# Moving the memory products of a gated attention kernel to the ends of its projection tiles, and making one of them from float32r halves

## The chip, the cores and the metric

The kernel runs on one core of one Trainium2 chip. A core has five engines that each work through a queue of their own in order: TensorE (PE, with its weight loads shown apart as PEld), VectorE (DVE), ScalarE (ACT), GpSimd (POOL) and SyncE (SP), which here only issues DMAs. Work on different engines is ordered by semaphores. The metric is the device time of one execution in microseconds.

## The reference: what is computed

For an input x of 2048 rows and 512 columns the reference computes two attentions with 32 heads of size 16 each, and mixes their outputs with a sigmoid gate per row.

```python
g = _sigmoid((x * gate_w).sum(-1, keepdims=True))
a = _A_ref(x, A_wqkv, A_wo)                 # full softmax attention over all 2048 rows
b = _B_ref(x, B_wq, B_wk, B_wv, B_wo, B_beta)
return g * a + (1 - g) * b
```

Side B works in four segments of 512 rows. Within a segment it is causal-block softmax attention; beside that each head keeps a memory M (16 x 16) and z (16) over the earlier segments:

```python
pq = phi(qs)                                 # phi(t) = t + 1 where t > 0, else exp(t)
num = jnp.einsum("bhld,bhde->bhle", pq, M)
den = jnp.einsum("bhld,bhd->bhl", pq, z)[..., None] + 1e-6
o = g * (num / den) + (1.0 - g) * a_dot      # this g is sigmoid(beta), per head
pk = phi(ks)
M = M + jnp.einsum("bhld,bhle->bhde", pk, vs)
z = z + jnp.einsum("bhld->bhd", pk)
```

The change concerns these memory products and two small loads: the gate's weights (`gw`) and `beta`.

## The kernel before

The program has two parts. The first projects x to queries, keys and values of side A, then of side B, and keeps the memory. The second, from line 700 on, makes scores, exponentials, values and the output, and runs for most of the time.

The first part is laid out by hand in *slots*. A call of `slot` (L304) issues the 12 matmuls of one projected tile of 128 rows by 512: four depth steps with three products each, because every operand is split into a high and a low float32r half (float32r is float32 rounded so that TensorE multiplies it in one pass; the low half holds the rest). After every three matmuls comes a *place*, 0 to 3, where other work is issued that was posted for this slot and this place with `post(slots, place, f)` (that many slots from now) or `post_at`. Work of one place is issued in the order in which it was posted. Since every engine's queue is in order, a place fixes where an instruction stands in the queue of its engine.

Side B takes twelve slots for each chunk c of 512 rows: q tiles in slots 12c to 12c+3, v tiles in 12c+4 to 12c+7, k tiles in 12c+8 to 12c+11. The texts below count these slots from the first one of side B. `qk_tile` (L362) posts three steps for the slot after a tile's matmuls: `e0` at place 0 (ScalarE copies the bank to `full` and casts it to the half `q1`, GpSimd makes `mn`, the minimum with 0), `e1` at place 1 (VectorE makes the low half `q2`, ScalarE `ex` = exp(mn)), `e2` at place 2 (VectorE makes `ph`, that is phi). Then, for a tile o of four:

- `mem_q` (L508), two slots after the q tile at place 1, multiplies phi(q) with the block-diagonal memory `mbd`, a float32 product `num` on TensorE; ScalarE copies it to `am`, and SyncE sends it away. After the fourth tile `mem_den` (L518) makes `den` a slot later at place 1.
- `mem_k` (L530), two slots after the k tile at place 1, transposes phi(k) on TensorE (`tps`), ScalarE copies that to `pt`; `mem_k2` (L538) at place 3 of the same slot makes the product `mps` with the values; `mem_k3` (L546) at place 0 of the next slot adds it on VectorE to the running `mrun` and makes `mbd` and `zbd`.

The banks of `num`, `den`, `tps` and `mps` come from one pool of two PSUM banks, `me_ps`, handed out in turn. `pt` and `am` share one buffer.

The second part needs the row maxima of the scores. The first 96 parts of them are made early, in the first part: `some_max` (L556) stands at place 3 of slots 14 to 19, 24 to 31 and 36 to 45, ahead of what is posted there later, and issues four maxima products `sm` on TensorE, which use half of its rows each, into four banks, with a reduction each on VectorE (L226). When the 64 maxima of the first side A unit are done, `finish_max` (L179) turns them with `nm` on VectorE and two `ms` operations on GpSimd. `gate_logit` (L471) is a VectorE product `jk` for the output gate, four for each chunk; its scratch is the buffer of `mn`.

Query tiles of the second part come from the pool `qp` (L94) with six buffers; three units are loaded in the first part. `gw` and `beta8` are loaded by GpSimd's DMA queue at the start (L454, L456).

Of the kernel before, what the change touches and what calls it, by code (L numbers as in the profile page):

```python
# [10 lines left out]
F32 = mybir.dt.float32  # L11
F32R = mybir.dt.float32r
# [7 lines left out]
D = 512  # L20
H = 32
DH = 16
CH = 512
NCH = S // CH
KT = D // 128
NG = 8
NO = 4
# [20 lines left out]
def gated_mix(ctx, tc, x, xT, wqkv, a_wo, b_wq, b_wk, b_wv, b_wo, beta, gate_w, out):  # L48
    nc = tc.nc
# [29 lines left out]
    bmask = const.tile([128, 8, DH], F32, name="bmask")  # L79
# [7 lines left out]
    gh = const.tile([128, NO], F32, name="gh")  # L87
# [189 lines left out]
    with ExitStack() as p0:  # L277
# [23 lines left out]
        def post(slots, place, f):  # L301
            posted.setdefault((now[0] + slots, place), []).append(f)
# [13 lines left out]
        def post_at(n, place, f):  # L316
            posted.setdefault((n, place), []).append(f)
# [133 lines left out]
        wAk = halves(wp, "wk", wqkv[:, D:2 * D], None, 2, [None, pairs[0]])  # L451
        wAv = halves(wp, "wv", wqkv[:, 2 * D:3 * D], 1, 4, [early[1].rearrange("p (k d) -> p k d", k=2), pairs[1]])
        gw = wk1.tile([128, D], F32, tag="gw", name="gw")
        nc.gpsimd.dma_start(gw, gate_w.unsqueeze(0).broadcast_to([128, D]))  # L454
        beta8 = wk1.tile([8, NO], F32, name="beta8")
        nc.gpsimd.dma_start(beta8, beta.rearrange("(o h) -> h o", h=8))  # L456

        def betas():

# [39 lines left out]
            xc = xn  # L499

        mrun = [st.tile([128, 8, 17], F32, name=f"mrun{o}") for o in range(NO)]
        mbd = [st.tile([128, DH, 8], F32, name=f"mbd{o}") for o in range(NO)]
        zbd = st.tile([128, NO, 32], F32, name="zbd")
        nc.gpsimd.memset(zbd, 0.0)

        pqs = []

        def mem_q(o, c, pq):  # L508
            nps = me_ps.tile([128, CH], F32, tag="me", name="num")
            nc.tensor.matmul(nps, mbd[o].rearrange("p e h -> p (e h)"), pq, start=True, stop=True)  # L510
            am = wk.tile([128, CH], F32, tag="am", name="am", bufs=1)
            nc.scalar.copy(am, nps)
            nc.sync.dma_start(numd[c][:, o], am)
            pqs.append(pq)
            if o == NO - 1:
                post(1, 1, lambda: mem_den(c))

        def mem_den(c):  # L518

            dps = me_ps.tile([128, CH], F32, tag="me", name="den")  # L520
            for o in range(NO):
                nc.tensor.matmul(dps[32 * o:32 * o + 32], zbd[:, o], pqs[o], start=True, stop=True,
                                 tile_position=(0, 32 * o))
            pqs.clear()
            dn = wk1.tile([128, CH], F32, tag="dn", name="dn")
            nc.scalar.activation(dn, dps, AF.Identity, bias=eps)
            for o in range(NO):
                nc.sync.dma_start(dend[c][8 * o:8 * o + 8], dn[32 * o:32 * o + 8])

        def mem_k(o, c, pk, vs):  # L530
            tps = me_ps.tile([128, 4, 128], F32, tag="me", name="tps")
            for b in range(4):
                nc.tensor.transpose(tps[:, b], pk[:, b * 128:(b + 1) * 128], identf)
            pt = wk.tile([128, CH], F32, tag="am", name="pt", bufs=1).rearrange("p (b t) -> p b t", t=128)
            nc.scalar.copy(pt, tps)
            post(0, 3, lambda: mem_k2(o, c, pt, vs))

        def mem_k2(o, c, pt, vs):  # L538
            mps = me_ps.tile([128, 8, 17], F32, tag="me", name="mps")
            for b in range(4):  # L540
                nc.tensor.matmul(mps.rearrange("p (g h) e -> p g (h e)", g=2), pt[:, b],
                                 vs[:, 2 * o:2 * o + 2, b].rearrange("p g h e -> p g (h e)"),
                                 start=(b == 0), stop=(b == 3))
            post(1, 0, lambda: mem_k3(o, c, mps))

        def mem_k3(o, c, mps):  # L546
            if c == 0:
                nc.vector.tensor_copy(mrun[o], mps)
            else:
                nc.vector.tensor_add(mrun[o], mps, mrun[o])  # L550
            nc.vector.scalar_tensor_tensor(mbd[o].rearrange("p e h -> p h e"), mrun[o][:, :, 0:16], gh[:, o:o + 1], bmask,
                                           op0=ALU.mult, op1=ALU.mult)
            nc.vector.tensor_scalar_mul(zbd[:, o, 0:8], bmask[:, :, 0], mrun[o][:, 0, 16:17])


# [29 lines left out]
        for c in range(NCH):  # L585
            if c + 1 == NCH:
                load_gate(c)
                post(8, 2, gates)
            for o in range(NO):
                then = (lambda pq, o=o, c=c: post(1, 1, lambda: mem_q(o, c, pq))) if c else None  # L590
                qk_tile("B", wBq, xc, o, qd["B", o, c], then)
            if c + 1 < NCH:
                xn = halves(xp, "x", xchunk(c + 1), now[0], now[0] + 3)
            if c + 1 < NCH:
                post(2, 3, lambda c=c: load_gate(c))
            vs = v_tiles("B", wBv, xc, c)
            for o in range(NO):
                then = (lambda pk, o=o, c=c, vs=vs: post(1, 1, lambda: mem_k(o, c, pk, vs))) if c + 1 < NCH else None
                qk_tile("B", wBk, xc, o, kd["B", o, c], then)
            xc = xn  # L600
        while posted:
# [491 lines left out]
```

## Time and profile before

| what | value |
|---|---|
| median of 3 runs | 1781.45 us (1780.76 to 1781.96) |
| profiled execution | 1781.19 us |
| its span in the trace | 1779.4 us |
| first projection matmul | 6.2 us |
| side B's projections and memory products, with the early maxima | about 117 to 303 us |
| second part | from 303.6 us |
| TensorE busy in the span | 1770.9 us (100%) |
| VectorE / ScalarE / GpSimd busy | 88% / 81% / 36% |

Times of instructions are us from the start of the span. A timeline row gives the start, the duration, the engine, the line, the operation, out<-in and the count; in brackets stands the idle time of the engine before it and what ended that. Matmuls are pipelined, so their durations overlap: what a matmul costs is read from start to start. In the stage views each engine has its busy time and, in parentheses, its instructions.

### The profile page before, as it was taken

What the parts mean: (1) busy time and instruction counts of PE and PEld (TensorE: products, weight loads), DVE (VectorE), ACT (ScalarE), POOL (GpSimd) and SP (SyncE); (2) the same over time, 40 slices, a digit from 0 to 9 for tenths busy, and PEclk for the clock granted to TensorE, in tenths of its full rate; (3) what the DMA queues carried; (4) which work ended last, traced back from release to release, by engine and by line L of the source; (5) the groups of instructions that cost most, each with busy time, mean ns of one, the idle gap of its engine ahead of it and who ended that gap; (6) DMA issues with size and microseconds to landing.
All of it is one profiled execution on the core that took longest, in us unless ns stands there. A gap on an engine that the chain in (4) does not pass through costs nothing.

```text
span 1779.4 us, 40691 instructions
## 1 busy us (share of the span) xinstructions
PE 1770.9 (100%) x14945; PEld 912.0 (51%) x14945; DVE 1573.8 (88%) x3331; ACT 1436.8 (81%) x2752; POOL 641.6 (36%) x748
## 2 busy tenths in 40 slices
PE   9999999999999999999999999999999999999999
PEld 7887776444444444444444444444444444444444
DVE  4235777999999999999999999999999999999931
ACT  5455444888888888888888888888888888888884
POOL 3002222405161416443434343343434253425342
PEclk9999999999999999999999999999999999999999
DMA  7677556444453536554454545454535354534551
GB/s 248 214 231 244 186 196 190 122 110 134 120 160 106 144 112 176 146 141 133 131 139 123 146 128 146 128 146 122 152 105 160 113 140 117 155 110 141 142 163 61
DMA packets 141270, 261.55 MB, mean 147 GB/s; under 512 B 36328, under 2 KB 58888, under 8 KB 140560
## 3 DMA queue, kind: packets, MB, share of 16 engines
q1 hardware_dynamic: 139712, 257.55, 49.9%
q8 instruction: 119, 1.95, 0.5%
q0 software_dynamic: 1216, 1.14, 0.3%
q14 instruction: 79, 0.65, 0.1%
q10 hardware_dynamic: 144, 0.26, 0.1%
HBM read 174.39 MB, written 83.25 MB: 145 GB/s over the span
## 4 chain that ended last, share of the span: by engine, by line
PE 94%; DVE 2%; ACT 1%; DMA 1%; POOL 1%; issue 0%; SPq 0%; POOLq 0%; DVEq 0%
PE ops L797 33%; PE st L740 27%; PE sm L205 14%; PE pr L311 10%; PE ops L909 4%; PE ops L680 2%; PE sm L909 2%; POOL mn L378 1%; PE pr L401 1%; DVE pm L226 1%; PE num L510 0%; DMA qdB<-q 0%; ACT ex L385 0%; DVE q L381 0%; PE mt_ps L196 0%
## 5 line engine op out<-in xcount | busy, mean ns | idle before, releaser
L763 ACT ACTIVATE p<-st 128x512 f32<-128x512 f32 x2261 | 1189.2, 600 | 152.8 <-PE sm L205 105.9
L226 DVE TENSOR_REDUCE pm<-sm 128x1 f32<-128x512 f32 x2048 | 1280.4, 681 | 11.8 <-PE sm L205 11.6
L740 PE MATMUL st<-qA,kA 50*128 50x512 f32 x2014 | 663.3, 432 | 0.0
L205 PE MATMUL sm<-kA,qA 48*128 48x512 f32 x2048 | 659.0, 428 | 0.1
L797 PE MATMUL ops<-p,vA 128*17 128x128 f32 (+3 forms) x6432 | 551.9, 441 | 0.0
L740 PEld LDWEIGHTS st<-qA,kA 50*128 50x128 f32 x2014 | 327.5, 185 | 415.2 <-ACT p L763 371.2
L205 PEld LDWEIGHTS sm<-kA,qA 48*128 48x128 f32 x2048 | 330.5, 185 | 15.3 <-issue 7.1
L859 POOL TENSOR_TENSOR rcp<-rec,minus 128x32 f32<-128x32 f32 x43 | 234.3, 5449 | 75.9 <-DMA rec<-dend 71.3
L238 DVE CUSTOM_DVE_ANT_0 rest<-sm,mask 128x128 f32<-128x128 f32 (+3 forms) x512 | 246.8, 482 | 1.8 <-PE sm L205 0.5
L797 PEld LDWEIGHTS ops<-p,vA 128*17 128x17 f32 x6432 | 130.4, 96 | 215.4 <-issue 190.4
L744 POOL TENSOR_SCALAR_AFFINE_SELECT p<-p 128x512 f32<-128x512 f32 x128 | 79.7, 640 | 330.3 <-ACT p L763 325.9
L205 PE MATMUL sm<-kB,qB 48*128 48x128 f32 (+3 forms) x512 | 166.1, 384 | 0.0
L740 PE MATMUL st<-qB,kB 50*128 50x512 f32 (+1 forms) x495 | 109.2, 329 | 0.3 <-ACT mt L199 0.3
L381 DVE TENSOR_TENSOR q<-full,q 128x512 fp32r<-128x512 f32 x56 | 38.6, 689 | 75.3 <-ACT q L374 68.8
L740 PEld LDWEIGHTS st<-qB,kB 50*128 50x128 f32 x495 | 69.8, 186 | 59.5 <-ACT p L763 48.7
L797 PE MATMUL ops<-p,vB 128*17 128x128 f32 (+3 forms) x1504 | 87.5, 350 | 0.0
L205 PEld LDWEIGHTS sm<-kB,qB 48*128 48x128 f32 x512 | 79.9, 184 | 0.0
L187 POOL CAST ms<-nm 128x16 fp32r<-128x16 f32 x32 | 6.7, 210 | 201.3 <-DVE nm L183 199.4
L378 POOL TENSOR_SCALAR mn<-full 128x512 f32<-128x512 f32 x24 | 35.7, 1489 | 101.3 <-ACT full L373 80.9
L373 ACT COPY full<-pr 128x512 f32<-128x512 f32 x56 | 32.7, 584 | 42.9 <-PE pr L311 39.2
L187 POOL CAST ms<-pm 128x16 fp32r<-128x16 f32 x32 | 6.3, 198 | 128.4 <-DVE pm L238 128.3
L875 POOL TENSOR_TENSOR v<-v,inv 128x512 f32<-128x512 f32 x31 | 39.9, 1289 | 27.2 <-DMA inv<-rdA 23.6
(198 smaller groups left out, 1617.5 us busy)
## 6 DMA issues: line engine op xcount, KB each, us to landing
kA<-kdA SPq DMA_DIRECT2D x256, 128.0 KB
vA<-vdA SPq DMA_DIRECT2D x31, 544.0 KB
kA<-kdA SPq DMA_DIRECT2D x256, 64.0 KB
kdA<-q SPq DMA_DIRECT2D x32, 256.0 KB
qdB<-q SPq DMA_DIRECT2D x32, 256.0 KB
qA<-qdA SPq DMA_DIRECT2D x64, 128.0 KB
kdB<-q SPq DMA_DIRECT2D x32, 256.0 KB
qB<-qdB SPq DMA_DIRECT2D x64, 128.0 KB
```

The source lines that it names most:

```text
L205: nc.tensor.matmul(ps[:, n0:n0 + n], rows(qt[u][:, :, s * 128:(s + 1) * 128], h, 48), rows(k[:, :, k0:k0 + n], h, 48), start=True, stop=True)
L226: nc.vector.tensor_reduce(pm[:, h, s, kc:kc + 1], ps, axis=AX.X, op=ALU.max)
L238: rows_left.append(lambda h=h, s=s, n0=n0, w=w: nc.vector.tensor_tensor_reduce(out=tri["rest"][:, 0:w], in0=ps[:, n0:n0 + w], in1=tri["mas ...
L311: nc.tensor.matmul(ps, l(a, k), r(b, k), start=(n == 0), stop=(n == 11))
L378: nc.gpsimd.tensor_scalar_min(ph["mn"], full, 0.0)
L740: nc.tensor.matmul(ps[:, n0:n0 + CH - q0], rows(k[:, :, b * 128:(b + 1) * 128], h, 50), rows(q[:, :, q0:], h, 50), start=True, stop=True)
L744: nc.gpsimd.affine_select(out=x, in_=x, pattern=[[0, 4], [1, 128]], base=0, channel_multiplier=-1, compare_op=ALU.is_ge, fill=0.0)
L763: nc.scalar.activation(p[:, h], ps, AF.Exp, scale=SCALE)
L797: nc.tensor.matmul(ops[32 * h:32 * h + 17, q0:q0 + 128 * w], v[:, 17 * h:17 * h + 17], p[:, h, c0:c0 + 128 * w], start=(i == 0), stop=done ...
L859: eng.tensor_tensor(r, rec, minus, op=ALU.pow)
L875: eng.tensor_mul(k["v"], k["v"], k["inv"])
L909: yield lambda i=i, x=x, w=w: nc.tensor.matmul(ps, t[:, b, x], halved[side][:, o, w], start=start and i == 0, stop=stop and i == 2)
```

## The change

- `mem_den`, `mem_k` and `mem_k2` move to place 3: `den` from place 1 to place 3 of the slot after the last `num`, `tps` from place 1 to place 3 of its slot, and `mps` to place 3 of the slot after that (so `mem_k3` is a slot later too). Posted during the run of the slots, they stand behind `some_max`, which was posted before; `beside_max` posts `tps` in two steps, so that `mps` of a tile stands ahead of `tps` of the next.
- `num` is made from halves. For every q tile, a new step `halve_q` two slots after it at place 1 lets ScalarE cast phi(q) to a high half and GpSimd subtract that for the low half; `mem_q` follows three slots after the tile at place 2, with three float32r matmuls in place of one float32 product. `mem_k3` splits `mbd` on VectorE: one copy and one subtraction of 128 x 128 more. The halves lie in three buffers of `qp`; `mbd` is one tile for all four o.
- `beta8` is loaded at slot 8 and `gw` at slot 16 of the first part's count (from the first slot of side A).

```diff
--- before.py
+++ after.py
@@ -451,9 +451,9 @@
         wAk = halves(wp, "wk", wqkv[:, D:2 * D], None, 2, [None, pairs[0]])
         wAv = halves(wp, "wv", wqkv[:, 2 * D:3 * D], 1, 4, [early[1].rearrange("p (k d) -> p k d", k=2), pairs[1]])
         gw = wk1.tile([128, D], F32, tag="gw", name="gw")
-        nc.gpsimd.dma_start(gw, gate_w.unsqueeze(0).broadcast_to([128, D]))
         beta8 = wk1.tile([8, NO], F32, name="beta8")
-        nc.gpsimd.dma_start(beta8, beta.rearrange("(o h) -> h o", h=8))
+        post_at(8, 0, lambda: nc.gpsimd.dma_start(beta8, beta.rearrange("(o h) -> h o", h=8)))
+        post_at(16, 0, lambda: nc.gpsimd.dma_start(gw, gate_w.unsqueeze(0).broadcast_to([128, D])))
 
         def betas():
 
@@ -499,21 +499,34 @@
             xc = xn
 
         mrun = [st.tile([128, 8, 17], F32, name=f"mrun{o}") for o in range(NO)]
-        mbd = [st.tile([128, DH, 8], F32, name=f"mbd{o}") for o in range(NO)]
+        mbd = st.tile([128, DH, 8], F32, name="mbd")
+        pqh = [qp.tile([128, 2, CH], F32R, tag="q", name="pqh") for _ in range(2)]
+        mbh = qp.tile([128, 2, CH], F32R, tag="q", name="mbh").rearrange("p a (o m) -> p a o m", o=NO)
         zbd = st.tile([128, NO, 32], F32, name="zbd")
         nc.gpsimd.memset(zbd, 0.0)
 
         pqs = []
 
+        def beside_max(f):
+
+            post(0, 3, lambda: post(1, 3, f))
+
+        def halve_q(o, pq):
+            ph = pqh[o % 2]
+            nc.scalar.copy(ph[:, 0], pq)
+            nc.gpsimd.tensor_sub(ph[:, 1], pq, ph[:, 0].bitcast(F32))
+
         def mem_q(o, c, pq):
             nps = me_ps.tile([128, CH], F32, tag="me", name="num")
-            nc.tensor.matmul(nps, mbd[o].rearrange("p e h -> p (e h)"), pq, start=True, stop=True)
+            ph = pqh[o % 2]
+            for i, (a, b) in enumerate(((0, 0), (1, 0), (0, 1))):
+                nc.tensor.matmul(nps, mbh[:, a, o], ph[:, b], start=i == 0, stop=i == 2)
             am = wk.tile([128, CH], F32, tag="am", name="am", bufs=1)
             nc.scalar.copy(am, nps)
             nc.sync.dma_start(numd[c][:, o], am)
             pqs.append(pq)
             if o == NO - 1:
-                post(1, 1, lambda: mem_den(c))
+                post(1, 3, lambda: mem_den(c))
 
         def mem_den(c):
 
@@ -533,7 +546,7 @@
                 nc.tensor.transpose(tps[:, b], pk[:, b * 128:(b + 1) * 128], identf)
             pt = wk.tile([128, CH], F32, tag="am", name="pt", bufs=1).rearrange("p (b t) -> p b t", t=128)
             nc.scalar.copy(pt, tps)
-            post(0, 3, lambda: mem_k2(o, c, pt, vs))
+            post(1, 3, lambda: mem_k2(o, c, pt, vs))
 
         def mem_k2(o, c, pt, vs):
             mps = me_ps.tile([128, 8, 17], F32, tag="me", name="mps")
@@ -548,8 +561,11 @@
                 nc.vector.tensor_copy(mrun[o], mps)
             else:
                 nc.vector.tensor_add(mrun[o], mps, mrun[o])
-            nc.vector.scalar_tensor_tensor(mbd[o].rearrange("p e h -> p h e"), mrun[o][:, :, 0:16], gh[:, o:o + 1], bmask,
+            nc.vector.scalar_tensor_tensor(mbd.rearrange("p e h -> p h e"), mrun[o][:, :, 0:16], gh[:, o:o + 1], bmask,
                                            op0=ALU.mult, op1=ALU.mult)
+            m = mbd.rearrange("p e h -> p (e h)")
+            nc.vector.tensor_copy(mbh[:, 0, o], m)
+            nc.vector.tensor_sub(mbh[:, 1, o], m, mbh[:, 0, o].bitcast(F32))
             nc.vector.tensor_scalar_mul(zbd[:, o, 0:8], bmask[:, :, 0], mrun[o][:, 0, 16:17])
 
 
@@ -587,7 +603,7 @@
                 load_gate(c)
                 post(8, 2, gates)
             for o in range(NO):
-                then = (lambda pq, o=o, c=c: post(1, 1, lambda: mem_q(o, c, pq))) if c else None
+                then = (lambda pq, o=o, c=c: (post(1, 1, lambda: halve_q(o, pq)), post(2, 2, lambda: mem_q(o, c, pq)))) if c else None
                 qk_tile("B", wBq, xc, o, qd["B", o, c], then)
             if c + 1 < NCH:
                 xn = halves(xp, "x", xchunk(c + 1), now[0], now[0] + 3)
@@ -595,7 +611,7 @@
                 post(2, 3, lambda c=c: load_gate(c))
             vs = v_tiles("B", wBv, xc, c)
             for o in range(NO):
-                then = (lambda pk, o=o, c=c, vs=vs: post(1, 1, lambda: mem_k(o, c, pk, vs))) if c + 1 < NCH else None
+                then = (lambda pk, o=o, c=c, vs=vs: beside_max(lambda: mem_k(o, c, pk, vs))) if c + 1 < NCH else None
                 qk_tile("B", wBk, xc, o, kd["B", o, c], then)
             xc = xn
         while posted:
```

## The prediction

> **What bounds the kernel now.** I read the page's chain first, then the busy times by stage, then the first part's TensorE timeline.
>
> ```profile
> span 1779.4 us, 40691 instructions
> PE 94%; DVE 2%; ACT 1%; DMA 1%; POOL 1%; issue 0%; SPq 0%; POOLq 0%; DVEq 0%
> ```
>
> TensorE carries 94% of the chain. All that is changed stands in the first part, whose three hand-overs (k tiles of a chunk, then q tiles of the next) are these stages:
>
> ```profile
> core 0: us, PE busy (x) PEld busy (x) DVE busy (x) ACT busy (x) POOL busy (x), PEclk, DMA share, GB/s
> 139.20:188.50 49.30, 48.77 (x233) 35.09 (x233) 32.47 (x63) 26.71 (x47) 12.21 (x9) 1.00 0.69 222
> 188.50:239.10 50.60, 50.28 (x242) 35.53 (x240) 38.13 (x73) 23.66 (x42) 12.17 (x9) 1.00 0.54 183
> 239.10:290.60 51.50, 50.99 (x245) 35.68 (x243) 39.53 (x80) 22.35 (x40) 12.96 (x11) 1.00 0.58 187
> ```
>
> TensorE is at the wall in each, but VectorE is at 39.53 of 51.50 us in the last, and its work stands in bunches. The second part starts when the first ends and has nothing changed; whatever is won or lost is won or lost before 304 us.
>
> **What TensorE is spared.** The product `num`, now (start, duration, operation):
>
> ```profile
> 163.56 1.02 PE L510 MATMUL num<-ph,mbd 128*128 128x512 f32 x2
> 164.65 0.40 PE L311 MATMUL pr<-xl,wqh 128*128 128x512 f32 x1
> 164.88 0.39 PE L311 MATMUL pr<-xh,wqh 128*128 128x512 f32 x1
> ```
>
> A projection matmul of 128x512, also float32r, takes 0.23 us from start to start (164.65 to 164.88). From 163.56 to 164.65 are 1.09; less one projection that is 0.86 for `num`. Three float32r matmuls are 3 x 0.23 = 0.69. Twelve times 0.17 is 2.1 us less.
>
> The second term is waiting: `tps` in mid-tile comes before phi(k) is ready.
>
> ```profile
> 154.38 0.40 PE L311 MATMUL pr<-xh,wqh 128*128 128x512 f32 x1
> 155.25 0.63 PE L533 MATMUL tps<-identf,ph 128*128 128x128 f32 x4 [0.47 <-DVE ph L390]
> 155.95 0.39 PE L311 MATMUL pr<-xl,wqh 128*128 128x512 f32 x1
> 159.19 0.39 PE L311 MATMUL pr<-xh,wqh 128*128 128x512 f32 x1
> 160.09 0.39 PE L311 MATMUL pr<-xl,wqh 128*128 128x512 f32 x1
> ...
> PE tps L533 <- DVE ph L390: 1.1, 3, 0.5
> PE num L510 <- DVE ph L390: 0.2, 1, 0.2
> ```
>
> Between the outer projections of the first `tps` lie 1.57 us, of the second, which waits for nothing, 0.90: the wait costs 0.67 where the row says 0.47. The waits' list (us in total, times, longest) has 1.1 for three such, so about 1.6 on the path, one in each hand-over; `num` adds about 0.3 once. Two places and a group of maxima later, phi(k) is long there.
>
> Third, `den` goes behind the maxima:
>
> ```profile
> 281.12 0.39 PE L311 MATMUL pr<-wkh,xh 128*128 128x512 f32 x1
> 282.44 0.39 PE L311 MATMUL pr<-wkl,xh 128*128 128x512 f32 x1
> ...
> 283.37 0.40 PE L311 MATMUL pr<-wkh,xh 128*128 128x512 f32 x1
> 285.03 0.40 PE L311 MATMUL pr<-wkl,xh 128*128 128x512 f32 x1
> ...
> 276.29 0.40 PE L311 MATMUL pr<-wkh,xh 128*128 128x512 f32 x1
> 277.28 0.41 PE L196 MATMUL mt_ps<-identf,ms 128*32 128x128 f32 x2
> 277.95 0.40 PE L311 MATMUL pr<-wkl,xh 128*128 128x512 f32 x1
> ```
>
> Less two projections each (0.46), the maxima alone (281.12 to 282.44) cost 0.86, `den` (283.37 to 285.03) 1.20, and maxima followed by `mt_ps`, tiled in columns as `den` is, 1.20. So a small column-tiled group still pays 0.34 behind the maxima, and `den` there saves some 0.1 at most: 0.3 for three. `tps` and `mps` only change places. Nothing more is saved at the switch.
>
> Fourth, at the start, `gw` (256 KB) leaves the crowd of the first loads:
>
> ```profile
> 0.80 4.71 DMA raw<-wqkv
> 1.95 0.84 POOL L454 DMA_DIRECT2D gw<-gate_w  x1
> ```
>
> TensorE's first projection waits for that load. The issue of `gw` starts 1.15 us behind it, and 0.84 more goes into issuing, so it shares at most 5.51 - 2.79 = 2.7 of the 4.7 us. At an equal share with the four 256 KB loads that SyncE and ScalarE had issued by then, a fifth of that, 0.5, is the upper end; 0 is the lower. I take 0.2, since its data cannot flow at once. `beta`'s few bytes, and both later DMA issues on GpSimd's queue (0.84 us, ahead of nothing timed; used tens of us later), I cost at nothing. In sum, if nothing else binds: 2.1 + 1.6 + 0.3 + 0.3 + 0.2 = 4.5 us.
>
> **What is late next.** Four prices stand against it. The first is a bank. `mps` of a tile takes the bank that `mps` of the tile before leaves, which is free when VectorE has done `mrun`. That now stands a slot later in VectorE's queue, behind the gate's `jk`:
>
> ```profile
> 152.53 0.63 ACT L385 ACTIVATE ex<-mn 128x512 f32<-128x512 f32 x1 [0.84 <-POOL mn L378]
> 153.20 0.69 DVE L473 SCALAR_TENSOR_TENSOR jk<-xg,gw 128x512 f32<-128x512 f32 x1 [1.28 <-ACT ex L385]
> 155.02 0.68 DVE L473 SCALAR_TENSOR_TENSOR jk<-xg,gw 128x512 f32<-128x512 f32 x1
> 155.63 0.29 DVE L548 COPY mrun<-mps 128x136 f32<-128x136 f32 x1
> ```
>
> This chain (`mn`, `ex`, `jk`, the next `mn`) doesn't hang on what moves, so it keeps its times. In the first hand-over TensorE, without maxima there and with `tps` behind the tile, gets to the second `mps` at about 154.8: slots 10 and 11 start at 144.8 and 148.0, slot 12 at 152.1 (12 x 0.23 each, `tps` 0.44, `mps` 0.93), its projections end at 154.8. But `mrun` of the first tile, behind the second `jk`, runs from 155.6 to 155.9. TensorE waits 1.2 us: one wait takes the place of the other. In the later hand-overs the maxima at this place (0.86) cover it.
>
> The second is the maxima's banks. Four reductions of slot n free the four banks of slot n + 1.
>
> ```profile
> 206.33 0.63 ACT L385 ACTIVATE ex<-mn 128x512 f32<-128x512 f32 x1 [0.92 <-POOL mn L378]
> 207.00 0.69 DVE L390 SCALAR_TENSOR_TENSOR ph<-full,ex 128x512 f32<-128x512 f32 x1 [0.69 <-ACT ex L385]
> 207.60 2.48 DVE L226 TENSOR_REDUCE pm<-sm 128x1 f32<-128x512 f32 x4
> 210.00 0.29 DVE L550 TENSOR_TENSOR mrun<-mps,mrun 128x136 f32<-128x136 f32 x1
> 210.32 0.48 DVE L551 SCALAR_TENSOR_TENSOR mbd<-mrun,gh,bmask 128x128 f32<-128x128 f32 x1
> ```
>
> The reductions of slot 24 are held by `ex` until 207.6 and end at 210.0, whatever TensorE does. Without its waits TensorE reaches the maxima of slot 25 at 209.1 (before: 211.1), and their last, due at 209.35, waits until 210.05: 0.7 back, in the second hand-over and, by the same order, in the third.
>
> The third is VectorE's new work: twelve copies and subtractions of 128x128. No row has them; the nearest, `mrun` (128x136, 0.32 to the next start), bounds each from above, and half of that from below. I take 0.5 for a pair: 6 us in all, 2 in each hand-over. In the first there are no maxima until slot 14, and `ex` is waited for meanwhile. In the other two a slot with `mrun`, `mbd`, `zbd` (0.73), `q2` and `ph` (0.6 each), four reductions (2.4) and the pair comes to 4.8, against 12 x 0.23 + 0.86 + 0.69 = 4.3 on TensorE once `num` runs: four such slots eat the slack and give 0.3 (0 to 1.2) back each.
>
> The fourth is GpSimd in the third hand-over. The new subtraction, 128x512 with two inputs, lies in its queue behind `mn`:
>
> ```profile
> 270.11 0.21 DVE L183 TENSOR_REDUCE nm<-pm 128x16 f32<-128x64 f32 x1
> 271.25 1.48 POOL L378 TENSOR_SCALAR mn<-full 128x512 f32<-128x512 f32 x1
> ...
> L644 POOL TENSOR_TENSOR wA<-wraw,wA 128x512 fp32r<-128x512 f32 x4 | 5.1, 1284 | 0.3
> ```
>
> `mn` waits there for `nm` through two `ms`; it ends at 272.7, the subtraction (1.28) at 274.0. TensorE, about 1 us earlier, wants that half at 273.4, and waits 0.6 to 1.1; I take 0.8. The twelve casts on ScalarE take the place where it waited for `num`, and cost nothing; elsewhere GpSimd has 4 us for 1.5 + 1.3.
>
> So 1.2 + 2 x 0.7 + 2 x 0.3 + 0.8 = 4.0 come back, and 4.5 - 4.0 = 0.5 stay. The SyncE issues of `am` and `den` move about a slot with their data, and the loads behind them are for maxima six slots ahead. The profiled execution, 1781.19, would be 1780.7; the median stands 0.26 above, at 1780.9. The range of this case alone is 1778 to 1783.
>
> **The rivals.** *The gains stay* (faster). The pool hands out its banks otherwise than in turn, and the new VectorE work hides under its waits. All of 4.5 is kept, or 5 with the whole of the start: 1776.5 to 1777. For it speaks TensorE's share of the chain; against it the times of `ex`, which nothing changed shortens.
>
> *GpSimd holds up VectorE* (slower). `mbd` took 0.81 beside a running `mn` and 0.48 without:
>
> ```profile
> 204.81 1.49 POOL L378 TENSOR_SCALAR mn<-full 128x512 f32<-128x512 f32 x1 [3.40 <-DVE jk L473]
> 204.88 0.81 DVE L551 SCALAR_TENSOR_TENSOR mbd<-mrun,gh,bmask 128x128 f32<-128x128 f32 x1
> 205.63 0.68 DVE L381 TENSOR_TENSOR q<-full,q 128x512 fp32r<-128x512 f32 x1
> ```
>
> If the new subtraction stops VectorE's two-input work for all of its 1.28 us, the eight in the two tight hand-overs cost up to 10 us, less the 2 us or so of slack: 1789. Slower by 0.2% (3.6 us, about what a measurement can tell from no change) begins when each takes over half of that from VectorE, 4.1 + slack 2 in eight. Against it: `q2`, two inputs from SBUF, took its usual 0.68 inside that `mn`. The Trainium skill ("SBUF — State Buffer", section "Who interferes with whom") has it that a DVE instruction with two SBUF inputs and a GpSimd instruction that reads SBUF exclude each other for a whole instruction; the row of `q2` disagrees, that of `mbd` agrees in part, and no row here has a two-input GpSimd operation beside such work.
>
> *The halves cost more than the product* (no change, or a little slower): pairs at 0.64 and a wait at each `num` of the third hand-over, 3 us more: 1784.
>
> **How the numbers follow.** Forecast with its terms as sized, and the third rival: 0.50 and 0.07, within 0.2% but for a small tail; the gains stay: 0.28; VectorE held up: 0.15. Faster 0.29, same 0.53, slower 0.18. The range 1776 to 1785.5 takes in the first rival and leaves out most of the second.
>
> **What would show it.** Right: three `num` matmuls 0.23 apart; no `tps` waiting for `ph`, but `mps` of the first hand-over waiting for `mrun`, and maxima of slots 25 and 37 waiting for reductions; the first part ending between 301 and 305. Wrong: that end before 300 or after 306, `q` and `mbd` on VectorE stretched beside GpSimd's subtractions, or a second part whose length changes by more than 1 us.

## The result and the profile after

The changed kernel takes 1785.41 us (median of 10 runs, 1784.26 to 1788.42) where the kernel before, run beside it, takes 1781.62 (1780.76 to 1782.48). The ratio is 1.0023, 95% interval 1.0014 to 1.0031: 3.8 us slower. The forecast was 1780.9 and no measurable change. The profiled execution took 1786.22 us.

The page of the changed kernel, its span, its chain of waits and the largest group of maxima products:

```profile
span 1784.5 us, 40750 instructions
...
PE 90%; DVE 4%; DMA 2%; ACT 2%; issue 1%; POOL 1%; SPq 0%; POOLq 0%; ACTq 0%; DVEq 0%
...
L205 PE MATMUL sm<-kA,qA 48*128 48x512 f32 x2048 | 665.8, 429 | 1.4
```

VectorE's share of the chain went from 2% to 4%, TensorE's from 94% to 90%. TensorE still does nearly everything, but more often something else ended last. Where the second part begins says in which part the time was lost. The first `st` matmul of the kernel before, then of the changed one:

```profile
303.58 0.50 PE L740 MATMUL st<-qA,kA 50*128 50x512 f32 x1
```

```profile
308.39 0.50 PE L756 MATMUL st<-qA,kA 50*128 50x512 f32 x1
```

The first part ends 4.8 us later, the span is 5.1 longer: the second part is as it was (0.3 longer). The three hand-overs, cut at the same times as those of before (they lie up to 4 us earlier in the work, since the kernel is late by then):

```profile
core 0: us, PE busy (x) PEld busy (x) DVE busy (x) ACT busy (x) POOL busy (x), PEclk, DMA share, GB/s
139.20:188.50 49.30, 48.22 (x231) 36.55 (x229) 37.11 (x70) 27.36 (x48) 17.32 (x13) 1.00 0.70 222
188.50:239.10 50.60, 50.10 (x239) 36.85 (x236) 40.48 (x78) 25.13 (x45) 17.26 (x13) 1.00 0.49 174
239.10:290.60 51.50, 50.51 (x240) 36.47 (x239) 43.01 (x87) 24.43 (x45) 17.86 (x15) 1.00 0.52 179
```

VectorE's busy time rises by 4.64, 2.35 and 3.48 us in them, 10.5 in all, and GpSimd's by 15.1. TensorE's records go down in each window: it gets less done. What it waits for stands in the list of waits (us in total, times, longest) from 139.2 to 305 us, before and after:

```profile
PEld sm L205 <- DVE pm L226: 0.4, 1, 0.4
```

```profile
PEld sm L205 <- DVE pm L226: 8.3, 22, 0.4
...
PEld num L523 <- POOL pqh L517: 0.9, 1, 0.9
PE num L523 <- POOL pqh L517: 0.5, 1, 0.5
PEld tps L546 <- DVE mrun L561: 0.2, 1, 0.2
```

The waits of `tps` for `ph` are gone, as forecast. But where one maxima product waited for a bank that a reduction holds, 22 do now. What they cost is read from start to start: a group's price is the time from the projection ahead of it to the second one behind it, less two projections (0.23 each), since the first one behind can start early in the record. Four maxima cost 0.86 when nothing is late. In the changed kernel single groups cost 1.12, 1.89, 1.52, 2.21 and 1.30, and two groups with `mps` and `tps` behind them 3.35 each where 2.22 is the price without a wait; the one with `mt_ps` cost 2.78, and 1.20 before. Summed over the whole first part, from these starts:

| us on TensorE | before | after |
|---|---|---|
| `num` x12 | 10.79 | 8.93 |
| `tps`, `mps`, `den`, maxima, `mt_ps` | 42.89 | 48.51 |
| both | 53.68 | 57.44 |

So `num` gains 1.9, the rest loses 5.6, and 3.8 is the measured loss. Two other things move the start of the second part, and both differ from kernel to kernel without following the change: side B starts at 117.0 us before and 117.8 after (116.6 to 118.1 in the kernels below), and one projection near 139 us waits for a late load (0.61 before, 1.04 after, at most 1.88 in those below). That is why the two profiled executions lie 5.0 us apart, and the medians 3.8.

VectorE's own groups (busy us, mean ns of one | idle time ahead and what ended it), 139 to 310 us, show why its reductions are late. Before, then after (there with GpSimd's subtraction):

```profile
L390 DVE SCALAR_TENSOR_TENSOR ph<-full,ex 128x512 f32<-128x512 f32 x24 | 16.6, 690 | 15.1 <-ACT ex L385 15.1
...
L551 DVE SCALAR_TENSOR_TENSOR mbd<-mrun,gh,bmask 128x128 f32<-128x128 f32 x12 | 7.8, 650 | 0.4
...
L553 DVE TENSOR_SCALAR zbd<-bmask,mrun 128x8 f32<-128x8 f32 x12 | 2.4, 204 | 0.0
```

```profile
L390 DVE SCALAR_TENSOR_TENSOR ph<-full,ex 128x512 f32<-128x512 f32 x24 | 17.0, 709 | 3.6 <-ACT ex L385 3.6
L517 POOL TENSOR_TENSOR pqh<-ph,pqh 128x512 fp32r<-128x512 f32 x12 | 15.5, 1294 | 16.2 <-ACT pqh L516 16.2
...
L564 DVE SCALAR_TENSOR_TENSOR mbd<-mrun,gh,bmask 128x128 f32<-128x128 f32 x12 | 8.4, 699 | 0.4
...
L567 DVE CAST mbh<-mbd 128x128 fp32r<-128x128 f32 x12 | 6.1, 511 | 0.4
L568 DVE TENSOR_TENSOR mbh<-mbd,mbh 128x128 fp32r<-128x128 f32 x12 | 4.5, 375 | 0.4
L569 DVE TENSOR_SCALAR zbd<-bmask,mrun 128x8 f32<-128x8 f32 x12 | 4.2, 346 | 0.0
```

The pair is 0.51 + 0.38 = 0.89 us, not 0.5, and `zbd` and `mbd` grew by 0.14 and 0.05. VectorE's idle time ahead of `ph` is down from 15.1 to 3.6: the slack on which the forecast counted is used up. A stretch of the first hand-over shows how the means come about:

```profile
163.80 1.49 POOL L378 TENSOR_SCALAR mn<-full 128x512 f32<-128x512 f32 x1 [1.78 <-ACT full L373]
164.01 0.67 DVE L564 SCALAR_TENSOR_TENSOR mbd<-mrun,gh,bmask 128x128 f32<-128x128 f32 x1
164.71 0.65 DVE L567 CAST mbh<-mbd 128x128 fp32r<-128x128 f32 x1
165.25 1.28 POOL L517 TENSOR_TENSOR pqh<-ph,pqh 128x512 fp32r<-128x512 f32 x1
...
165.40 1.28 DVE L568 TENSOR_TENSOR mbh<-mbd,mbh 128x128 fp32r<-128x128 f32 x1
166.58 1.49 POOL L378 TENSOR_SCALAR mn<-full 128x512 f32<-128x512 f32 x1
166.60 0.62 DVE L569 TENSOR_SCALAR zbd<-bmask,mrun 128x8 f32<-128x8 f32 x1
```

With GpSimd at rest, at 212 us, the same four take 0.45, 0.23, 0.29 and 0.23. Here the cast is 0.65 beside `mn`, and the subtraction of 128x128 takes 1.28, as long as the GpSimd subtraction beside it.

### The profile page after: what moved, and what is told of

The parts are those of the page before. It is cut to its first block, busy times and chain, and to the rows that moved or that the text cites. A ratio compares the mean times of both kernels' runs of the same rounds, so it can differ in the third digit from the quotient of the medians.

```text
span 1784.5 us, 40750 instructions
## 1 busy us (share of the span) xinstructions
PE 1775.2 (99%) x14957; PEld 920.4 (52%) x14957; DVE 1587.3 (89%) x3355; ACT 1441.4 (81%) x2764; POOL 656.2 (37%) x760
## 4 chain that ended last, share of the span: by engine, by line
PE 90%; DVE 4%; DMA 2%; ACT 2%; issue 1%; POOL 1%; SPq 0%; POOLq 0%; ACTq 0%; DVEq 0%
PE ops L813 33%; PE st L756 27%; PE sm L205 14%; PE pr L311 7%; PE ops L925 4%; PE ops L696 2%; PE sm L925 2%; DVE pm L226 2%; DVE q L381 1%; PE pr L401 1%; DVE ph L390 1%; POOL mn L378 1%; DMA raw<-xT 0%; DVE mbd L564 0%; ACT full L373 0%
## 5 line engine op out<-in xcount | busy, mean ns | idle before, releaser
L205 PE MATMUL sm<-kA,qA 48*128 48x512 f32 x2048 | 665.8, 429 | 1.4
L205 PEld LDWEIGHTS sm<-kA,qA 48*128 48x128 f32 x2048 | 334.1, 185 | 20.9 <-DVE pm L226 8.7
```

Of the source, the lines that this page charges most:

```text
L205: nc.tensor.matmul(ps[:, n0:n0 + n], rows(qt[u][:, :, s * 128:(s + 1) * 128], h, 48), rows(k[:, :, k0:k0 + n], h, 48), start=True, stop=True)
```

## The experiments

The theory after this reading: VectorE's queue in the hand-overs is too full for the pair, and GpSimd's subtraction makes VectorE's instructions longer; the moves and `num` gain what was forecast. The rivals: the moves themselves cost (a bank, a buffer), the later loads cost, or the new work costs time wherever it stands. In the table, the sum of the groups is the one above (without the wait for the load); 53.68 is the kernel before.

| kernel | median us | ratio to before, 95% | sum of groups |
|---|---|---|---|
| changed kernel | 1785.41 | 1.0023 (1.0014 to 1.0031) | 57.44 |
| e1 moves alone | 1785.86 | 1.0028 (1.0017 to 1.0040) | 57.90 |
| e2 halves alone | 1785.75 | 1.0029 (1.0017 to 1.0040) | 57.02 |
| e3 later loads alone | 1781.79 | 1.0001 (0.9992 to 1.0009) | 53.63 |
| e4 GpSimd memset | 1782.69 | 1.0007 (0.9999 to 1.0016) | 54.75 |
| e5 pair elsewhere | 1802.64 | 1.0121 (1.0105 to 1.0136) | 70.3 |
| e6 no pair | 1781.22 | 1.0000 (0.9991 to 1.0008) | 52.84 |
| e7 neither | 1778.02 | 0.9982 (0.9973 to 0.9991) | 50.89 |
| e8 moves, `num` late | 1780.53 | 0.9996 (0.9988 to 1.0005) | 52.89 |
| e9 new work later | 1790.87 | 1.0054 (1.0042 to 1.0067) | 60.1 |
| e10 the same, old places | 1788.62 | 1.0039 (1.0026 to 1.0051) | 58.3 |
| e11 before + GpSimd's work | 1782.12 | 1.0004 (0.9995 to 1.0013) | 53.88 |
| e12 before + pair | 1783.54 | 1.0011 (1.0002 to 1.0020) | 55.50 |
| e13 maxima shifted | 1790.14 | 1.0041 (1.0028 to 1.0054) | 55.96 |
| e14 before, maxima shifted | 1788.98 | 1.0042 (1.0029 to 1.0054) | 57.27 |
| e15 copy late on ScalarE | 1781.80 | 1.0002 (0.9994 to 1.0011) | 53.55 |
| e16 one-input GpSimd | 1783.28 | 1.0014 (1.0005 to 1.0023) | 55.73 |
| e17 `zbd` there too | 1781.14 | 0.9995 (0.9986 to 1.0004) | 52.58 |
| e18 split at place 3 | 1786.33 | 1.0026 (1.0016 to 1.0035) | 58.2 |

Seven of these traces differ from the others in the granted TensorE clock. Up to the last 4 us of an execution it is 1.00 in the kernel before, in the changed one and in the rest; in these seven it stands at 0.50 for a while, which costs TensorE at most half of that time: in e2 for 6.8 us from 278.6, in e5 for 20.5 us in four stretches between 172 and 295, in e10, e17 and e18 for 3.4 us each between 276 and 291, in e13 for 3.4 us at 283 and 13.7 at 310, in e14 for 3.4 at 311. What lowered it, no run here shows.

**Which part of the change: e1, e2, e3, e8.** The three parts alone, each with the rest as before:

```diff
# e1: before, with
-                post(1, 1, lambda: mem_den(c))
+                post(1, 3, lambda: mem_den(c))
-            post(0, 3, lambda: mem_k2(o, c, pt, vs))
+            post(1, 3, lambda: mem_k2(o, c, pt, vs))
-                then = (lambda pk, o=o, c=c, vs=vs: post(1, 1, lambda: mem_k(o, c, pk, vs))) if c + 1 < NCH else None
+                then = (lambda pk, o=o, c=c, vs=vs: beside_max(lambda: mem_k(o, c, pk, vs))) if c + 1 < NCH else None
# e2: the changed kernel with these three and the loads undone
# e3: before, with
-        nc.gpsimd.dma_start(gw, gate_w.unsqueeze(0).broadcast_to([128, D]))
-        nc.gpsimd.dma_start(beta8, beta.rearrange("(o h) -> h o", h=8))
+        post_at(8, 0, lambda: nc.gpsimd.dma_start(beta8, beta.rearrange("(o h) -> h o", h=8)))
+        post_at(16, 0, lambda: nc.gpsimd.dma_start(gw, gate_w.unsqueeze(0).broadcast_to([128, D])))
```

> The moves alone: den, tps and mps at the tile's end, num still one float32 product at its old place, both loads at the start. If the moves lose by themselves (waits for the mrun bank and for the maxima's banks), this is 2 us or more slower than before, 1783.6 or later. If VectorE's and GpSimd's new work is the cause, the moves alone are within 1 us of before: 1.9 us of waits for phi go, 1.2 + 2 x 0.7 us of waits for mrun and for the maxima come, den wins 0.3: 1781 to 1782.5.

> The halves alone: num from float32r halves as in the changed kernel, while den, tps and mps stand where they stood before and both loads stay at the start. If VectorE and GpSimd are the cause, the maxima of the second and third hand-over wait as in the changed kernel, some 4 to 6 us, against 2.1 us won on num: 1783 to 1786. If the moves are the cause, the 2.1 us show: 1779 to 1780.5.

> The later loads of gw and beta alone, all else as before. In the profiles side B starts 0.8 us later after the change, with 0.4 us of that by the 18th us, and the wait at 139 us grows by 0.4. If the later loads cause that, this is 1 to 1.4 us slower than before; if it is chance, it is within 0.5 us, or 0.2 us faster as forecast.

The loads do nothing that the runs can tell from nothing. Each of the other two alone is as slow as both, e2 in part by the clock: that is worth up to 3.4 of its 4.2 us, and its one run at a mean clock of 1.000 took 1783.98. Of e1 the theory had expected no loss, so that is a miss. Its reason stands in the waits and in one stretch of e1:

```profile
ACT am L516 <- PE mps L545: 10.9, 3, 3.7
...
PE num L514 <- DVE ph L390: 3.4, 4, 1.8
```

```profile
166.94 0.58 ACT L516 COPY am<-num 128x512 f32<-128x512 f32 x1 [3.56 <-PE mps L545]
167.43 0.64 ACT L385 ACTIVATE ex<-mn 128x512 f32<-128x512 f32 x1
...
168.09 0.69 DVE L390 SCALAR_TENSOR_TENSOR ph<-full,ex 128x512 f32<-128x512 f32 x1 [3.91 <-ACT ex L385]
...
168.84 1.13 PE L514 MATMUL num<-ph,mbd 128*128 128x512 f32 x2 [0.54 <-DVE ph L390]
```

`am` and `pt` are one buffer. The later `mps` holds `pt`, so ScalarE stands 3.56 us at `am`; `ex` and `ph` stand behind it, and the next `num` waits for `ph`. Twelve `num` cost 15.77 instead of 10.79. In the changed kernel `num` comes five places later and misses this. e8 is e1 with only that added, and float32 as before:

```diff
-                then = (lambda pq, o=o, c=c: post(1, 1, lambda: mem_q(o, c, pq))) if c else None
+                then = (lambda pq, o=o, c=c: post(2, 2, lambda: mem_q(o, c, pq))) if c else None
```

> The moves as in e1_moves, with num still a float32 product but at its new place, slot 3 and place 2 behind the tile. In e1 the copy of num waited for pt's buffer, which num's copy shares and which is read a slot later than before; ScalarE stood 3.6 us and phi(q) came late, 5.4 us of waits at num. If that order is why e1 was slow, the waits at num go: 1780.5 to 1782. If the moves cost by the banks of the maxima, 1783.5 or later.

Twelve `num` at 0.86 with no wait, and 52.89 in all: the moves with a late `num` save 0.8 by the trace, 0.5 by the runs, which is no more than can be told from nothing. Two groups of maxima cost 2.98 and 2.95 instead of 2.22: they wait 0.75 each, without any new work.

**Which part of the new work: e4, e6, e7, e11, e12.** Taken from the changed kernel (e4 the subtraction, e6 the pair, e7 both), and added to the kernel before as work that nothing uses (e11 the subtraction, e12 the pair):

```diff
# e4
-            nc.gpsimd.tensor_sub(ph[:, 1], pq, ph[:, 0].bitcast(F32))
+            nc.gpsimd.memset(ph[:, 1].bitcast(F32), 0.0)
# e6
-            nc.vector.scalar_tensor_tensor(mbd.rearrange("p e h -> p h e"), mrun[o][:, :, 0:16], gh[:, o:o + 1], bmask,
+            nc.vector.scalar_tensor_tensor(mbh[:, 0, o].rearrange("p (e h) -> p h e", h=8), mrun[o][:, :, 0:16], gh[:, o:o + 1],
...
-            nc.vector.tensor_copy(mbh[:, 0, o], m)
-            nc.vector.tensor_sub(mbh[:, 1, o], m, mbh[:, 0, o].bitcast(F32))
# e7: both
# e11: before, with
+                (post(1, 1, lambda: nc.gpsimd.tensor_sub(pqh[o % 2][:, 1], pq, pq)), post(1, 1, lambda: mem_q(o, c, pq)))
# e12: before, with, in mem_k3 after mbd
+            nc.vector.tensor_copy(mbh[:, 0, o], m)
+            nc.vector.tensor_sub(mbh[:, 1, o], m, mbh[:, 0, o].bitcast(F32))
```

> The changed kernel with GpSimd's subtraction for the low half of phi(q) replaced by a memset of the same 128x512 buffer: the low half of phi(q) is left out of num. A memset reads nothing from SBUF and takes half as long. If GpSimd's subtraction holds up VectorE, the long ones of the changed kernel go (mbh subtraction 1.28, mbd 1.12, ph 1.26 us) and 2 us or more come back: 1783.4 or earlier. If the pair on VectorE alone is the cause, its cast still takes 0.6 us beside mn, and under 1 us comes back: 1784.5 to 1785.5.

> The changed kernel without the pair: VectorE's product writes the high half of the memory itself, and the low half stays zero, so num lacks the memory's low half. VectorE has then the same instructions as before the change. If its new work is the cause, the maxima's waits fall by more than half: 1780 to 1782.5. If GpSimd's subtraction holding VectorE up is as large a part, under 2 us come back: 1783.5 or later.

> Both taken away: no pair on VectorE, and a memset in place of GpSimd's subtraction (num lacks both low halves). What stays is the moves, the three float32r matmuls, ScalarE's cast and the later loads. If the new work of VectorE and GpSimd is the whole cause, the gains of the moves and of num show, 2 to 3 us: 1778.5 to 1780. If the moves cost by themselves through the banks, it stays at 1781 or later.

> The kernel before with twelve GpSimd subtractions of 128x512 added (phi(q) minus itself into a free query buffer that nothing reads), at the place of the change's halve_q. If GpSimd's subtraction alone holds VectorE up enough to matter, the single VectorE instructions beside it stretch to up to 1.28 us and the kernel loses 1.5 to 3 us: 1782.5 to 1784. If it matters only together with the pair, it is within 0.7 us of before.

> The kernel before with the pair on VectorE added (the memory's halves into a free query buffer that nothing reads). If VectorE's queue is the bound of the hand-overs by itself, 2 to 4 us are lost: 1783 to 1785. If before has the slack that the forecast gave it (0.3 us back in each hand-over), 1781.5 to 1782.

Without the pair the loss of 3.8 is gone; without both the kernel is 3.1 us faster than before, close to the gains of the forecast (4.5) less the two waits of 0.75. So the pair costs some 4 us, and the subtraction 2.6 (after to e4) to 3.2 (e6 to e7, where the sums of the groups say 2.0). Waits of the maxima, e6 and then e7:

```profile
PEld sm L205 <- DVE pm L226: 5.0, 14, 0.4
```

```profile
PEld sm L205 <- DVE pm L226: 3.2, 10, 0.4
```

Added to the kernel before, they cost less: 2.2 for the pair, and for the subtraction 0.8 +- 1.6, which the runs can't tell from nothing. The pair's cost in e12 is in `num` (12.64 against 10.79; one waits 1.48 for `ph`), and in no maxima. In the changed kernel TensorE reaches the maxima earlier, for `tps` no longer holds it up. That `num` waits in e12 and the maxima in the changed kernel is read from the traces; that the earlier maxima make the difference in price is argued, not tried by itself.

**How the new work costs: e16, e5, e15, e17.** e16 replaces GpSimd's subtraction (1.29 us) by an operation with one input on the same tile, which takes longer:

```diff
-            nc.gpsimd.tensor_sub(ph[:, 1], pq, ph[:, 0].bitcast(F32))
+            nc.gpsimd.tensor_scalar_min(ph[:, 1], pq, 0.0)
```

> The changed kernel with GpSimd's two-input subtraction (1.29 us) replaced by an operation with one input on the same tile (as mn, 1.49 us); the low half of phi(q) is then not the reference's. If GpSimd's time in its own queue is what costs: 1785 to 1786. If it is the exclusion of VectorE's two-input instructions by a two-input one: as with the memset, 1782.5 to 1783.5.

With the one-input operation 1.5 of the 3.8 us come back (57.44 to 55.73 in the sum), with the memset 2.6. So about half of the subtraction's cost or more is that it stretches VectorE, not GpSimd's queue (each median carries an interval of about 1.6 us to either side, so the runs alone leave the 1.5 open; the sums of the groups, 1.7, agree with it). Beside the one-input operation (1.48 to 1.49 long) `mbd` took 0.45 twice, beside the subtraction 1.12 and 1.11.

e5 takes the pair off VectorE at the same place; e15 moves the copy to ScalarE, a slot later and behind `ex`, and the subtraction, which stays on VectorE, to the slot after that; e17 moves `zbd` with the copy:

```diff
# e5
-            nc.vector.tensor_copy(mbh[:, 0, o], m)
-            nc.vector.tensor_sub(mbh[:, 1, o], m, mbh[:, 0, o].bitcast(F32))
+            nc.scalar.copy(mbh[:, 0, o], m)
+            nc.gpsimd.tensor_sub(mbh[:, 1, o], m, mbh[:, 0, o].bitcast(F32))
# e15 (and four mbd tiles)
+            post(1, 2, lambda: nc.scalar.copy(mbh[:, 0, o], m))
+            post(2, 1, lambda: nc.vector.tensor_sub(mbh[:, 1, o], m, mbh[:, 0, o].bitcast(F32)))
# e17: e15, with
-            nc.vector.tensor_scalar_mul(zbd[:, o, 0:8], bmask[:, :, 0], mrun[o][:, 0, 16:17])
+            post(1, 2, lambda: nc.scalar.mul(zbd[:, o, 0:8], bmask[:, :, 0], mrun[o][:, 0, 16:17]))
```

> The changed kernel with the pair that splits the memory taken off VectorE: ScalarE casts the high half, GpSimd subtracts for the low one (128x128 each). If VectorE's queue is the bound of the hand-overs, the cast's 0.3 to 0.6 us and the subtraction's 0.3 to 1.3 leave it, and 2 to 4 us come back: 1781.5 to 1783.5. If the order of GpSimd's and ScalarE's work is the cause, this adds to both: 1785 or later.

> The changed kernel with only the pair's copy on ScalarE, a slot later at place 2, so that it doesn't stand ahead of the next tile's full as in the run with the pair elsewhere; the subtraction stays on VectorE, a slot after that (four mbd tiles). VectorE's work: 0.51 of 0.89 us of each pair goes, so 2 to 3 of the pair's 4.2 us come back: 1782.5 to 1783.5. If ScalarE is held up by VectorE again: above 1786.

> As the run with the pair's copy late on ScalarE (1781.8), and zbd (128x8, 0.35 us each in the changed kernel, 1.29 beside GpSimd's subtraction) goes to ScalarE at the same place. Theory (VectorE's queue between the reductions sets the maxima): 4.2 us of VectorE's work go, of which half or so was waited for: 1779.5 to 1781. If only the copy counted: 1781.5 to 1782.5.

e5 is the slowest of all, 17.2 us behind the changed kernel. Up to 10.2 of that can be the clock at 0.50; its waits show another reason:

```profile
POOL mbh L568 <- ACT mbh L567: 46.9, 12, 5.0
ACT mbh L567 <- DVE zbd L569: 37.5, 12, 4.5
```

At place 0 the copy stands ahead of the next tile's `full` in ScalarE's queue and waits there 3.1 us on average for VectorE, so everything behind `full` is late. A slot later it waits for nothing and takes 0.29 us, and some 3 us come back (e15). So most of the pair's cost goes when the copy, 6.1 of VectorE's 10.6 new us, leaves VectorE and the subtraction comes later; which of the two moves gives how much was not tried apart. With `zbd` gone too, e17 stands 0.5 us below before, within its interval (the sum of groups: 1.1 below). Of the versions that compute everything e8 and e17 are the best, and neither can be told from the kernel before.

**Elsewhere in time: e9, e10, e13, e14, e18.** e9 puts the pair, the split of phi(q) and `num` two to three slots later, with `den` at its old place; e10 has `tps` and `mps` at their old places beside that. e13 and e14 take the early maxima off the q tiles, in the changed kernel and in the one before. e18 is e15 with the split of phi(q) at place 3.

```diff
# e9
+            post(3, 0, lambda: halve_m(o))
...
-(post(1, 1, lambda: halve_q(o, pq)), post(2, 2, lambda: mem_q(o, c, pq)))
+(post(3, 1, lambda: halve_q(o, pq)), post(4, 2, lambda: mem_q(o, c, pq)))
# e13, e14
-        for n in range(14, 64):
-            if n // 12 > 2 or n % 12 < 8:
+        for n in range(16, 64):
+            if n // 12 > 3 or n % 12 >= 4:
# e18
-(post(1, 1, lambda: halve_q(o, pq)), post(2, 2, lambda: mem_q(o, c, pq)))
+(post(1, 3, lambda: halve_q(o, pq)), post(2, 3, lambda: mem_q(o, c, pq)))
```

> All of the new work is kept and put where VectorE has room: the pair that splits the memory three slots after mem_k3, phi(q)'s halves two slots later than in the changed kernel, num five slots after its tile, so that they fall on the v tiles' slots; mbd is four tiles again, den stands a slot after the last num at place 1, both loads at the start. tps and mps at the tile's end as in the change. If the new work costs only because it stands in the hand-overs, num's 2.1 us and the 0.5 us of the moves show: 1777.5 to 1779.5. If it costs wherever it stands (GpSimd excluding VectorE), 1781 or later.

> As e9, with tps and mps at their old places. If the moves of tps and mps are worth the 0.5 us that e8_moves_late_num suggests, this is 0.5 us slower than e9: 1778.5 to 1780. If they only trade one wait for another, it equals e9 within 0.3.

> The changed kernel with the early maxima taken off the hand-overs: slots 16 to 23, 28 to 35 and 40 to 47 in place of 14 to 19, 24 to 31 and 36 to 45, so that no reductions stand in VectorE's queue beside the memory's pair. If the loss is VectorE's bunch in the hand-overs, the waits of the maxima there go (in the changed kernel 1.0 + 0.7 + 1.4 + 0.4 alone and 2 x 1.1 ahead of mps) and the time falls from 1785.4 to 1779 to 1781. If the new work costs its time wherever it stands, 1784 to 1786.

> The kernel before with the same shift of the early maxima. It has no waits of maxima to lose; the reductions now stand among the k tiles, whose phi(k) is late already for tps: 1781.5 to 1783. If this is as fast as the shifted changed kernel, the shift pays by itself and the change adds nothing.

> As the run with the pair's copy late on ScalarE (1781.8), and the split of phi(q) stands at place 3 in place of 1, num a place later (3 in place of 2), so that GpSimd's subtraction runs more beside the reductions and less beside VectorE's two-input work. If the exclusion costs by where the subtraction stands: 1779.5 to 1781. If it only moves to the next tile's mn, ex and ph: 1782 to 1784.

None of the five is faster than the kernel before, and none came out as expected, except that e9 lies in the open range (1781 or later) of its second branch. e10 is 2.2 us faster than e9, where at most 0.5 slower was expected: so with the halves late, moving `tps` and `mps` costs rather than saves. In e9 the `num` products find all they need (0.67 to 0.68 each), but ScalarE stands at `am` until the DMA of the tile before has left the shared buffer, and a projection then waits for `full` (2.3 of the 9.6 us lost; 6.4 stand in the groups):

```profile
196.40 0.59 ACT L525 COPY am<-num 128x512 f32<-128x512 f32 x1 [5.92 <-DMA numd<-am]
...
197.52 0.50 PE L311 MATMUL pr<-xh,wvl 128*128 128x512 f32 x1 [2.09 <-ACT full L373]
```

In e14 the reductions make phi(k) late and `tps` costs 12.06 in place of 7.12; in e13 two groups of `mps` and `tps` cost 3.81 and 3.48 in place of 1.36 (`tps` waits up to 2.4 for `mrun`), and in both the second part is longer, by 5.5 and 2.5 us. The clock can account for the first: it stands at 0.50 from 310.3 to 324.0, worth up to 6.8 us; in e14 it is worth up to 1.7 of the 2.5, and the rest stays open. Three of e13's five runs have a mean clock of 0.995 (1790.14 to 1791.22), the other two 0.999 (1784.95 and 1785.38), and at those it is no slower than the changed kernel. With that shift the changed kernel's first part ends as that of the kernel before (308.09 and 308.02), and its groups cost 1.3 less (55.96 against 57.27). So away from the reductions of the hand-overs the change loses nothing, as the theory has it, but the shift itself costs 3.6 in the groups of the kernel before. In e18 the subtraction pushes back the next tile's `mn`: `ex` waits 41.6 us for `mn` in all, 30.3 in e15, so `ph` and the reductions are late, and one group of maxima and `num` costs 4.44 where 1.56 is the price. So these five don't settle whether there is a better place; they show that none of the places tried is free.

## Why the prediction was wrong

**The gains came.** `num` costs 0.67 to 0.69 in 11 of 12 (forecast 0.69); no `tps` waits for `ph`; `den` with maxima is 1.85 against 0.86 + 1.20, so 0.2 is saved each where 0.1 was forecast. The start's 0.2 is below what e3 can show. e7, which leaves the new work out, is the sum of these less what the moves give back.

**The first price, the bank**, was too large and at the wrong instruction: forecast 1.2 at the second `mps` of the first hand-over. That `mps` waits for nothing; the `tps` behind it waits 0.24 for `mrun` of the first tile, and the third `mps` 0.31 for `mrun` of the second, which ends at 160.70 (1.60 and 1.67 for `mps` and `tps`, against 1.36). So the bank that the first `mps` left fell to a `tps` and not to the second `mps`: the order of the banks was taken from the pool's description and not from a row.

**The second price, the maxima of slots 25 and 37**, was right: forecast 0.7 each, 0.75 in e7 and e8.

**The third price is the step that failed.** The pair was put at 0.5, between 0.32 and 0.64, with 0.3 given back in each of two hand-overs and nothing in the first. It took 0.89, above the upper end, and gave back some 4 us, of which 1.3 in the first hand-over (two groups of maxima at 1.12 and 1.89 instead of 0.86; without the pair, in e6, none waits there). Three things were wrong in it. The bound came from `mrun`, which takes 0.29 whatever GpSimd does; but beside a one-input `mn` the cast takes 0.65 to 0.68, at which the rows of `mbd` (0.81 and 0.48) had already hinted. The slack was counted by the slot (4.3 against 4.8), though the second price just above had found the reductions late by 0.7 with no new work. And four slots that are over by 0.5 make 2.0 in a hand-over; the forecast took 0.3 of that, for a slack to which it gave no row. So over a third of the new work on VectorE was not hidden: some 4 us were lost to 10.6 us of it.

The sum had a second gap beside this one. It held no term for VectorE standing still beside GpSimd's subtraction; that was left to the rival below. The subtraction cost 2.6 us (e4), about half of it or more in this way (e16).

**The fourth price** was right in place and size: `num` of the third hand-over waits for `pqh` behind `nm` and `mn`, 0.8 forecast, 1.43 - 0.68 = 0.75 measured.

**The rival "GpSimd holds up VectorE"** (0.15) was half true. It put the point of decision at half of 1.28 us taken in each of eight subtractions. In the changed kernel `mbd` lost 0.67 and 0.66, the 128x128 subtraction 0.99 and `ph` 0.57, each once; no other two-input instruction was stretched so. The Trainium skill ("SBUF — State Buffer", section "Who interferes with whom") says that a VectorE instruction with two SBUF inputs and a GpSimd instruction that reads SBUF exclude each other for a whole instruction. Beside GpSimd's two-input subtraction the trace now agrees (1.12, 1.28 and 1.26 beside 1.28 to 1.43). Beside the one-input `mn` it agrees only in part: the 128x128 subtraction took 0.29 in the three cases of the changed kernel, which began 0.72 to 0.76 behind the start of `mn`, and 0.61 to 0.71 in five cases of e13, e15 and e16 that began 0.06 to 0.15 behind the start of a one-input operation; none of them was held for the whole of it. The row of `q2` on which the prediction leaned began 0.82 behind the start of its `mn` (205.63 against 204.81), so it could not show this.

**Signs named beforehand.** The end of the first part, 308.39, is past the 306 from which the forecast was to count as wrong; `mbd` and `ph` were stretched beside the subtraction (`q` was not); the second part kept its length.

## What to carry over

Before work is added to an engine's queue, look up in the trace what releases the bound engine at that place: if a transfer of buffers from the crowded engine is already the last releaser, the new work is not hidden there, however idle the engine is on average (here some 4 of 10.6 us were lost). Take such durations from rows in which the neighbours run as they will in the changed kernel. And when a consumer is moved later, look at what its buffer shares: here the same move lost 4 us or gained a little, depending on whether the copy into the shared buffer was moved along.

## What the runs showed of the hardware

A VectorE cast of 128x128 float32 took 0.21 to 0.23 us with GpSimd at rest and, in the changed kernel, 0.65 to 0.68 when it began behind the middle of a one-input GpSimd operation (1.49), ending 0.07 to 0.09 after it; the three that began 0.09 to 0.33 behind its start took 0.40 to 0.60 and ended while it still ran. The two-input subtraction of the same size took 0.29 alone and when it began 0.72 to 0.76 behind the start of that operation; the five that began 0.06 to 0.15 behind it (e13, e15, e16) took 0.61 to 0.71 and ended 0.73 to 0.74 before it did, as here in e16:

```profile
215.97 1.48 POOL L378 TENSOR_SCALAR mn<-full 128x512 f32<-128x512 f32 x1
216.11 0.61 DVE L568 TENSOR_TENSOR mbh<-mbd,mbh 128x128 fp32r<-128x128 f32 x1
```

So what GpSimd's one-input operation costs a VectorE instruction depends on when in it the instruction begins; the reason is not shown here. And size is no protection beside a two-input GpSimd operation. `zbd`, 128 partitions of 8 numbers, took 0.2 us in the kernel before, and in e15:

```profile
214.87 1.28 POOL L517 TENSOR_TENSOR pqh<-ph,pqh 128x512 fp32r<-128x512 f32 x1
214.89 1.29 DVE L569 TENSOR_SCALAR zbd<-bmask,mrun 128x8 f32<-128x8 f32 x1
```
